# Batch 0's pooling ordered by when its loads land, output evictions shared between two engines, and a new work list

## The chip, the cores and the metric

The kernel runs on one core of a Trainium2 chip. The metric is the device time of one execution in microseconds. A core has a matrix engine (TensorE, PE in the profile, with its weight loads as PEld), three engines that read and write on-chip memory (VectorE or DVE, ScalarE or ACT, GpSimd or POOL), a queue engine (SyncE or SP) and 16 DMA engines. Engines run in their own order and wait for each other through semaphores. Matrix results go to PSUM, which has eight banks of 128 x 512 fp32 values; DVE or ACT takes them from there ("evicts" them) to SBUF.

## The reference

Four batches of 12544 rows of x with 128 features pass through an attention with 32 inducing points and then through a maxout layer:

```python
def mab(q, kv):
    s = scale * (q @ kv.transpose(0, 2, 1))
    s = s - s.max(-1, keepdims=True)
    a = np.exp(s)
    a /= a.sum(-1, keepdims=True) + 1e-09
    return a @ kv
h = mab(I, x)                  # per batch: 32 x 128, pooling over 12544 rows
attn = mab(x, h)               # 12544 x 128 again
h1, h2 = attn @ w1, attn @ w2  # 128 -> 1024
out = np.maximum(h1, h2) @ w_out
```

The output is 50176 x 128 in fp32.

## The kernel before, in words

**The algebra.** The second attention gives each row as a sum of 32 rows of h with weights e / sum(e), so `attn @ w` is `e @ (h @ w)` over the same sum. The kernel writes max(h1, h2) as relu(h2 - h1) + h1. Per batch it makes `hwd` = h (w2 - w1), 32 x 1024, and `m1` = h w1 w_out, 32 x 128. A row of the output is then (relu(e hwd) w_out + e m1) / sum(e).

**Tiling.** A batch is 98 chunks of 128 rows. Blocks take four "quarters" of up to four chunks each; quarter q lives on partitions 32q to 32q+31. `stage` (L625) computes the 32 scores of each chunk of a block into one bank, and ACT's exponential (L637) writes them as `e2`. A "phase" (`phase`, L1009) is up to four jobs, one for each quarter, that run side by side in the four 32-row strips of PE: a job multiplies `e2` by a part of `hwd` into a bank of its own, and a relu on ACT (L1024) or DVE (L1027) takes the bank to SBUF. A phase can also carry the "linear" part of a group, `e2` times `m1`, straight into the output's bank. A "group" is one quarter of one block: eight final matmuls for each chunk (L859) add relu times w_out up in one bank. Then `evict_group` multiplies by 1 / sum(e) while it writes fp32 to one of `NOUT` output buffers (L891, DVE), and SP issues the store (L918). The sums of e come from a DMA transpose and POOL's adds (`turn_e2`, L651 to L664), for the first blocks from a small matmul (`dens`, L704).

**Batch 0's pooling** runs ahead of all that, since nothing else is there to do. Its 98 chunks come in 11 loads, of 14 (four), 7 (four), 6, 5 and 3 chunks. The first part comes in fp32 over SP's queue, the others as fp16 over POOL's, followed by w1, w2 and w_out. For part i, `p1_transpose` turns the chunks on PE (L262) into two banks, of which DVE (L266) copies the first and ACT (L269) the second; `p1_scores` multiplies with the inducing points (L278), ACT takes the exponential (L287), and `p1_accum` adds up sums (L301) and h (L310). Nine warm-up matmuls run before the first load lands (L728), and `fill` puts in seven more (L720), whose results nobody reads: two inside part 0, then two, two and one behind parts 0, 1 and 2. Behind pooling come w1's negation (`w1h` times -1, DVE, L768), `small_h` (L455 on DVE, L465 on ACT), `weights_2` (eight transposes of w1, L562, copied by DVE, L565, and ACT, L568), `small_sums` (L481), the first `stage`, `small_hwd` (L501, L502, evicted by DVE, L509, and ACT, L516) and `weights_3` (L575). Pooling of batches 1 to 3 is spread through the work of the batch before, with DMA transposes of x on SP's queue (L200).

**What sets the order.** All five engines run in the order of the program text (`manual_schedule`). From L1035 on that is a list of words written out: a number is so many final matmuls, `p4.5` a phase of up to four jobs with a mask that flips the engine of its relus, `s` a stage, `gN` the sums of block N, `xB.J`, `cB.J`, `tB.J`, `aB.J` the steps of batch B's pooling, `HWmo` the small steps of batch 0's weights. While the program is built, a `Clock` keeps estimates of when each engine is free and each bank is released. With them it picks the bank for a tile, which jobs a phase takes and, but for the mask, whether ACT or DVE takes a relu:

```python
if (max(ck.act, ready) + 0.477 <= max(ck.dve, ready) + 0.597) != bool(flip >> k & 1):
    nc.scalar.activation(out=dst, in_=src, func=AF.Relu)
```

Nothing of the clock is in the program that runs, only the choices made with it. `on_act` and `on_dve` hold the entry for each instruction, `on_sp` and `st[b]["ld", i]` those for stores and loads.

Of the kernel before, what the change touches and what calls it, by code (L numbers as in the profile page):

```python
# [17 lines left out]
NOUT = 5  # L18


class Clock:
# [4 lines left out]
    LAT = 0.20  # L26
    SEM = 0.05

    def __init__(self):
        self.pe = self.act = self.dve = self.sp = 0.0  # L30
        self.pool = self.loading = self.loaded = 0.0
        self.stored = [0.0] * NOUT
        self.mode = "full"
        self.bank = [0.0] * 8
        self.idle = {}
        self.log = []
        self.busy = {}
# [86 lines left out]
def kernel(  # L124
# [57 lines left out]
    def load_x(b, i, after=None):  # L182
        k0, n = parts[b][i]
        if after is not None:

            nc.gpsimd.tensor_copy(out=pace, in_=after)
        nc.gpsimd.dma_start(out=xn_at[b, i][:, 0:n, :], in_=xr[b, :, k0 : k0 + n, :])  # L187
        if b:
            if i == 0:
                ck.loading = ck.pe  # L190
            ck.on_pool(ck.pe, 0.55)
            st[b]["ld", i] = ck.loaded = max(ck.pe, 14.0) + 8.0 + 2.7 * i
# [24 lines left out]
    w1h = relup.tile([128, 4096], F16, name="w1h", tag="relu1")[:, 0:J]  # L217
    w21 = consts.tile([C, J], F16, name="w21")
    woutp = consts.tile([128, NJB, C], F16, name="woutp")
    w1T = consts.tile([128, NJB, C], F16, name="w1T")  # L220
# [6 lines left out]
    with tc.manual_schedule(engines={ET.PE, ET.DVE, ET.Activation, ET.Pool, ET.SP}):  # L227
# [25 lines left out]
        def p1_transpose(b, i, between=0):  # L253
            k0, n = parts[b][i]
            xn = xn_at[b, i]
            h = min(8, (n + 2) // 2)
            for g, m in ((0, h), (h, n - h)):
                if g and between:
                    fill(between)
                bi, ps = bank([128, 8, 128], F16)  # L260
                for j in range(m):
                    nc.tensor.transpose(ps[:, j, :], xn[:, g + j, :], identity16)  # L262
                end = ck.run(0.056 * m, ready=ck.bank[bi], why="T")
                dst = xT_tiles[b % 2][:, k0 + g : k0 + g + m, :]
                if g == 0:
                    nc.vector.tensor_copy(out=dst, in_=ps[:, 0:m, :])  # L266
                    ck.bank[bi] = ck.on_dve(end, 0.08 + 0.075 * m)
                else:
                    nc.scalar.copy(out=dst, in_=ps[:, 0:m, :])  # L269
                    ck.bank[bi] = ck.on_act(end, 0.05 + 0.12 * m)  # L270
                st[b]["xT", i] = max(ck.bank[bi], st[b].get(("xT", i), 0.0))

        def p1_scores(b, i):
# [11 lines left out]
            end = ck.run(0.029 * n)  # L285
# [5 lines left out]
        def p1_accum(b, i, lo=0, hi=P1):  # L291
# [4 lines left out]
            if b == 0:  # L296
# [20 lines left out]
                st[0]["end"] = ck.run(0.029 * (hi - lo) + 0.03 * ((hi - lo + 3) // 4))  # L317
# [132 lines left out]
        def small_h(b):  # L450
            hT4 = smp.tile([C, 4, M], F16, name=f"hT4_{b}", tag="hT4")
            if b == 0:
# [9 lines left out]
                st[b]["hT4r"] = ck.on_dve(st[0]["end"], 0.3)  # L462
# [3 lines left out]
                ready = ck.on_act(st[0]["end"], 0.2)  # L466
# [10 lines left out]
        def small_sums(es, ready):  # L477
# [9 lines left out]
            ck.bank[st[0]["eb"]] = st[0]["rsr"] = ck.on_dve(end, 0.34)  # L487

        def small_hwd(b, halves=(0, 1), vector=False):
# [3 lines left out]
            for half in halves:  # L493
                for n in range(2 if b == 0 and half == 0 else 1):
# [25 lines left out]
                    st[b]["hw", half] = max(ck.bank[bi], st[b].get(("hw", half), 0.0))  # L520
# [35 lines left out]
        def weights_2():  # L556
            for g in range(2):
                bi, ps = bank([128, 4, 128], F16)
                ck.wait(ck.bank[bi], "w")
                for j in range(4):  # L560
                    jb = 4 * g + j
                    nc.tensor.transpose(ps[:, j, :], w1h[:, 128 * jb : 128 * (jb + 1)], identity16)  # L562
                end = ck.run(0.056 * 4)
                if g == 0:
                    nc.vector.tensor_copy(out=w1T[:, 0:4, :], in_=ps)  # L565
                    ck.bank[bi] = ck.on_dve(end, 0.4)
                else:
                    nc.scalar.copy(out=w1T[:, 4:8, :], in_=ps)  # L568
                    ck.bank[bi] = w_of["w1T"] = ck.on_act(end, 0.5)
# [162 lines left out]
        for i in range(4):  # L732
            p1_transpose(0, i, 2 if i == 0 else 0)
            if i < 3:
                fill(2 - i // 2)
            if i == 0:
                bi, ps = bank([128, 512])
                nc.tensor.transpose(ps[:, 0:M], ind_sb, identity32[0:M, 0:M])
                nc.vector.tensor_copy(out=inducingT, in_=ps[:, 0:M])
                ck.bank[bi] = 0.0  # L740
                nc.vector.reduce_sum(out=diag, in_=identity32.rearrange("p (k m) -> p m k", m=M), axis=AX.X)
                for dst, f in ((rep32, DOWN / scale), (repd, 1.0)):
                    nc.vector.tensor_scalar(
                        out=dst.rearrange("p (k m) -> p k m", m=M),
                        in0=diag[:, None, :].broadcast_to((128, 4, M)),
                        scalar1=f,
                        scalar2=None,
                        op0=ALU.mult,
                    )
            if i > 0:  # L750
                p1_accum(0, i - 1)
            p1_scores(0, i)
        last = len(parts[0]) - 1
        p1_transpose(0, 4)
        p1_accum(0, 3)
        p1_transpose(0, 5)
        p1_scores(0, 4)
        for i in range(6, last + 1):
            p1_transpose(0, i)
            p1_scores(0, i - 1)  # L760
            p1_accum(0, i - 2)
        p1_scores(0, last)
        p1_accum(0, last - 1)
        p1_accum(0, last)
# [3 lines left out]
        nc.vector.tensor_scalar(out=w1h, in0=w1h, scalar1=-1.0, scalar2=None, op0=ALU.mult)  # L768
        sums = small_h(0)
        weights_2()  # L770
        small_sums(*sums)
        stage(blocks[0])
        small_hwd(0, (0,))

# [8 lines left out]
        for n, g in enumerate(groups):  # L783
            g.blk.last_group[g.q] = n
        state.update({"g": 0, "mm": 0, "done": 0, "issued": 0})
# [95 lines left out]
        def evict_group(g, end):  # L881
# [3 lines left out]
            qs = sorted({q for q, _ in g.chunks})  # L885
            per = n // len(qs)
            t0 = g.chunks[0][1]
            rp = g.blk.rp[:, t0 : t0 + per, qs[0] : qs[-1] + 1]
            if len(qs) == 1:
                rp = rp.broadcast_to((128, per, C))  # L890
                nc.vector.tensor_mul(osb[:, 0:n, :], g.ps[:, 0 : n * C].rearrange("p (s c) -> p s c", s=n), rp)  # L891
            elif per == 1:
                rp = g.blk.rp[:, t0, qs[0] : qs[-1] + 1]
                nc.vector.tensor_mul(
                    osb[:, 0:n, :],
                    g.ps[:, 0 : n * C].rearrange("p (s c) -> p s c", s=n),
                    rp[:, :, None].broadcast_to((128, n, C)),
                )
            else:
                for i, q in enumerate(qs):  # L900
                    nc.vector.tensor_mul(
                        osb[:, per * i : per * (i + 1), :],
                        g.ps[:, per * i * C : per * (i + 1) * C].rearrange("p (s c) -> p s c", s=per),
                        g.blk.rp[:, t0 : t0 + per, q : q + 1].broadcast_to((128, per, C)),
                    )
            end = max(end, g.blk.divided, ck.stored.pop(0))
            ck.bank[g.bank] = ck.on_dve(end, 0.066 + n * 128 / 960.0)
# [13 lines left out]
        def next_job(q):  # L921
# [11 lines left out]
            if ("hw", unit[3] // unit[2]) not in st[blk.b] or relu_slot(blk, q) is None:  # L933
# [26 lines left out]
        def phase(n, flip=0):  # L960
            gl, jobs = pick(n)
            got = []
            free = sorted(range(8), key=lambda j: ck.bank[j])
            ready = 0.0
            for (q, blk, unit), bi in zip(jobs, free):
                ready = max(ready, ck.bank[bi], blk.staged, st[blk.b]["hw", unit[3] // unit[2]])
                got.append((q, blk, unit, bi, bank([128, 512], only=bi)[1]))
            if ck.mode != "row":
                keep_busy(ready - ck.SWITCH["row"])
                ck.pe += ck.SWITCH["row"]  # L970
                ck.mode = "row"
            ck.wait(ready, "phase")
            parts_ = []
            if gl is not None:
                q, b = gl.q, gl.blk.b
                r = slice(32 * q, 32 * (q + 1))
                parts_.append((q, [
# [10 lines left out]
                ]))  # L988
            for q, blk, (_, t0, w, u), bi, ps in got:
# [3 lines left out]
                parts_.append((q, [  # L993
# [10 lines left out]
                ]))  # L1004
            parts_ = [seq for _, seq in sorted(parts_, key=lambda e: e[0])]
# [4 lines left out]
            end = ck.run(0.226, "row")  # L1010
            if gl is not None:
                gl.linear = True
                if gl in held:
                    held.remove(gl)
                    evict_group(gl, end)
            for k, (q, blk, (_, t0, w, u), bi, ps) in enumerate(got):
# [5 lines left out]
                ready = end + 0.03  # L1022
# [13 lines left out]
        H0 o p4.5 s W p4.2 s 4 m0 4 p2.1 3 p3.2 1 g2 4 p2 8 p3.3 p2 14 p3.1 4 p4.1 6 x1.0 16 p2.1 p4.10  # L1036
        16 x1.1 x1.2 p4.4 4 g1 12 p4.9 12 p4.11 p1 19 p3.4 p2 14 p4 s s 3 x1.3 x1.4 4 x1.5 x1.6 7 p3.5 s
        s g3 8 p4.10 27 p3 p4.2 18 p3.2 14 p3 6 p4.4 12 x1.7 3 x1.8 x1.9 c1.0 p1 p4.4 13 g4 1 p4.5 15
# [84 lines left out]
```

## Time and profile before

| | us |
|---|---|
| median of 3 runs (317.37 to 317.73) | 317.66 |
| the profiled execution | 318.49 |
| its span, first to last instruction | 316.7 |
| batch 0's pooling, first scores to last accumulation | 8.71 to 22.48 |
| first final matmul (L859) | 26.89 |
| PE busy over the span | 311.5 |
| ACT busy, DVE busy | 279.0, 273.6 |

An execution's time is 1.8 us longer than its span. The granted clock of PE is 1.00 throughout. A row of the page's costliest groups reads: line, engine, operation, output tile and input tiles, shapes, count, then busy time and mean nanoseconds of one, then how long the engine stood idle just before, and for what. A row of the timeline begins with its start and its length in us; rows of the chain of waits with the start and the length of a link.

### The profile page before, as it was taken

Reading aid. Unit: us, or ns where it says so; the run is one execution under the profiler, and the core shown is the slowest. Engines: PE = TensorE matmul, PEld = TensorE weight load, DVE = VectorE, ACT = ScalarE, POOL = GpSimd, SP = SyncE. Lnnn points to the kernel's source line nnn. Section 1 sums busy time; section 2 is a strip of 40 time slices with the busy share of each in tenths; the row PEclk is TensorE's granted clock in tenths of the full one; section 3 lists DMA queues with packets and bytes.
Section 4 is the critical chain, followed back from the end, with each engine's and each line's share of the span. In section 5 each row is a group of like instructions: output and inputs, shape, how many; then the busy total and the mean of one; then the engine's idle time right before and its main releaser. Section 6 shows DMA issues by size and latency. Waiting matters only on the chain.

```text
span 316.7 us, 12562 instructions
## 1 busy us (share of the span) xinstructions
PE 311.5 (98%) x5309; PEld 240.8 (76%) x5309; DVE 273.6 (86%) x486; ACT 279.0 (88%) x571; POOL 127.5 (40%) x189
## 2 busy tenths in 40 slices
PE   8999999999999999999999999999999999999996
PEld 3885767777877768778777787887868777787885
DVE  2348989999888899998988998889899989989995
ACT  2669999999999999998999989999899999998881
POOL 7442071648510066067320064449305663461500
PEclk9999999999999999999999999999999999999999
DMA  8999999999699998997399998995423233324223
GB/s 205 209 206 212 226 232 213 225 239 217 120 215 244 234 175 175 198 234 205 113 216 243 179 248 212 229 187 169 139 85 118 85 120 118 119 79 146 104 103 117
DMA packets 81480, 56.34 MB, mean 178 GB/s; under 512 B 62832, under 2 KB 66064, under 8 KB 81424
## 3 DMA queue, kind: packets, MB, share of 16 engines
q1 hardware_dynamic: 75312, 41.32, 56.6%
q0 software_dynamic: 6112, 14.22, 23.1%
q8 instruction: 41, 0.67, 1.0%
q14 instruction: 15, 0.12, 0.1%
HBM read 28.33 MB, written 25.69 MB: 171 GB/s over the span
## 4 chain that ended last, share of the span: by engine, by line
PE 95%; ACT 1%; DMA 1%; DVE 1%; issue 1%; DVEq 0%; ACTq 0%
PE ps L859 61%; PE ps L1009 23%; PE ps L625 2%; PE ps L262 2%; PE ps L338 2%; PE ps L396 1%; DMA xf<-in_x_dram 1%; PE ps L278 1%; PE ps L310 1%; PE ps L720 1%; PE ps L301 1%; PE ps L505 0%; PE ps L441 0%; ACT hwd L516 0%; ACT relu L1024 0%
## 5 line engine op out<-in xcount | busy, mean ns | idle before, releaser
L1024 ACT ACTIVATE relu<-ps 128x512 f16<-128x512 f32 x472 | 242.9, 619 | 20.8 <-PE ps L1009 18.9
L1027 DVE TENSOR_SCALAR relu<-ps 128x512 f16<-128x512 f32 x312 | 198.5, 684 | 19.4 <-PE ps L1009 18.6
L859 PE MATMUL ps<-woutp,relu 128*128 128x128 f16 x3136 | 204.0, 219 | 0.0
L859 PEld LDWEIGHTS <-relu 128*128 128x128 f16 x3136 | 176.6, 98 | 34.2 <-issue 28.7
L1009 PE MATMUL ps<-e,hwd 32*128 32x512 f16 (+2 forms) x880 | 85.3, 357 | 0.0
L660 POOL TENSOR_TENSOR half<-ed 128x256 f32<-128x256 f16 (+2 forms) x23 | 14.1, 613 | 126.9 <-DMA ed<-e 126.6
L664 POOL TENSOR_TENSOR rd<-den,minus 128x16 f32<-128x16 f32 (+2 forms) x23 | 60.7, 2639 | 1.9
L891 DVE TENSOR_TENSOR o<-ps,rd 128x512 f32<-128x512 f32 (+1 forms) x88 | 55.5, 633 | 4.1 <-PE ps L1009 2.4
L1009 PEld LDWEIGHTS <-hwd 32*128 32x128 f16 x880 | 28.0, 91 | 18.4 <-issue 5.1
L1009 PE MATMUL ps<-m,e 32*128 32x128 f16 x382 | 38.5, 216 | 0.0
L1009 PEld LDWEIGHTS <-e 32*128 32x128 f16 x382 | 22.6, 92 | 5.4 <-issue 1.7
L660 POOL TENSOR_TENSOR half<-half 128x32 f32<-128x32 f32 (+3 forms) x69 | 22.3, 323 | 5.4
L187 POOL DMA_DIRECT2D xn<-in_x_dram x31 | 17.0, 557 | 7.3 <-DMA xn<-in_x_dram 4.5
L891 DVE TENSOR_TENSOR o<-ps,rp 128x512 f32<-128x512 f32 (+3 forms) x20 | 12.9, 644 | 1.1 <-DMA out_dram<-o 0.8
L266 DVE COPY xT<-ps 128x512 f16<-128x512 f16 (+3 forms) x11 | 5.5, 504 | 8.3 <-PE ps L262 8.1
L637 ACT ACTIVATE e<-ps 128x512 f16<-128x512 f32 (+2 forms) x21 | 11.0, 596 | 0.2 <-PE ps L625 0.2
L351 ACT ACTIVATE eu<-ps 128x512 f16<-128x512 f32 x18 | 11.1, 615 | 0.1
L269 ACT COPY xT<-ps 128x768 f16<-128x768 f16 (+3 forms) x11 | 6.1, 557 | 3.6 <-PE ps L262 3.4
L625 PE MATMUL ps<-xT,hT 128*32 128x512 f16 (+3 forms) x114 | 8.8, 363 | 0.1
L262 PE MATMUL ps<-identity,xn 128*128 128x128 f16 x98 | 7.8, 226 | 0.1
L262 PEld LDWEIGHTS <-xn 128*128 128x128 f16 x98 | 6.0, 101 | 1.7 <-DVE xn L724 1.0
L338 PE MATMUL ps<-xT,inducingT 128*32 128x512 f16 x72 | 7.1, 386 | 0.0
(100 smaller groups left out, 112.4 us busy)
## 6 DMA issues: line engine op xcount, KB each, us to landing
out_dram<-o SPq DMA_DIRECT2D x90, 256.0 KB, 2.7
xn<-in_x_dram POOLq DMA_DIRECT2D x24, 448.0 KB, 11.8
out_dram<-o SPq DMA_DIRECT2D x10, 128.0 KB, 2.6
xn<-in_moe_w_dram POOLq DMA_DIRECT2D x4, 256.0 KB, 14.0
xn<-in_x_dram POOLq DMA_DIRECT2D x4, 224.0 KB, 9.6
xT<-xn SPq DMA_TRANSPOSE x33, 4.4
xf<-in_x_dram SPq DMA_DIRECT2D x1, 512.0 KB, 3.7
xf<-in_x_dram SPq DMA_DIRECT2D x1, 384.0 KB, 4.2
```

Source lines behind the costliest of these rows:

```text
L187: nc.gpsimd.dma_start(out=xn_at[b, i][:, 0:n, :], in_=xr[b, :, k0 : k0 + n, :])
L262: nc.tensor.transpose(ps[:, j, :], xn[:, g + j, :], identity16)
L338: nc.tensor.matmul(out=ps[32 * g : 32 * (g + 1), :], lhsT=inducingT, rhs=xT_tiles[b % 2][:, U * u + 4 * g : U * u + 4 * (g + 1), :], start ...
L351: nc.scalar.activation(out=eu, in_=ps, func=AF.Exp, scale=scale, accum_out=st[b]["es"][:, u : u + 1])
L625: nc.tensor.matmul(out=ps[32 * q : 32 * (q + 1), 128 * t : 128 * (t + n)], lhsT=hq, rhs=xT[:, c : c + n, :], start=True, stop=True, tile_p ...
L660: nc.gpsimd.tensor_tensor(out=dst, in0=cur[:, :, 0:n], in1=cur[:, :, n : 2 * n], op=ALU.add)
L664: nc.gpsimd.tensor_tensor(out=rp[:, 0:wd, :].rearrange("p t q -> p (t q)"), in0=den[:, 0 : 4 * wd], in1=minus1[:, 0 : 4 * wd], op=ALU.pow,)
L859: nc.tensor.matmul(out=g.ps[:, 128 * c : 128 * (c + 1)], lhsT=g.blk.relu[g.q][:, 128 * (jb * w4 + t) : 128 * (jb * w4 + t + 1)], rhs=woutp ...
L891: nc.vector.tensor_mul(osb[:, 0:n, :], g.ps[:, 0 : n * C].rearrange("p (s c) -> p s c", s=n), rp)
L1009: nc.tensor.matmul(**seq[i])
L1024: nc.scalar.activation(out=dst, in_=src, func=AF.Relu)
L1027: nc.vector.tensor_scalar(out=dst, in0=src, scalar1=0.0, scalar2=None, op0=ALU.max)
```

## The change

Five things change at once.

1. **Batch 0's pooling.** A list `HEAD` spells the order out: `3a` and `3b` are the two halves of part 3's transposes, `S3` its scores, `A3` its accumulation, `I` the transposes of the inducing points and the small DVE work on them. Transposes of a part stand where the clock has them landed (`LANDED`). Five of the seven idle matmuls are gone; the two inside part 0 stay.
2. **Between pooling and the list.** `weights_2` is cut in three: the first four transposes of w1 where all eight were, the other four behind the first half of `small_hwd`, and then the two copies. The transposed w1 lives in the relu buffer that also holds w1. The list now begins with `H1` instead of `H0`: hwd's second half stands before the first phase and is evicted by DVE instead of ACT.
3. **Evictions of the output.** For each of the 108 groups a character of `EVICT` names the engine: 0 is DVE in one instruction, as before; 1 is ACT, an instruction for each chunk, with the column of reciprocals as its scale. The string has 90 zeros and 18 ones; the 18 groups have 61 chunks. (2 would share a group out and does not occur.)
4. **Six output buffers** instead of five.
5. **The clock and the list.** The clock follows a phase's four strips one by one (`ROW`, `ck.tile`), knows hwd by pieces of 256 columns, and has some other entries changed. A phase issues the linear part first instead of by quarter. The list of words is new throughout: 250 phases instead of 249; PE changes between whole-array, row-strip and column-strip matmuls 342 times instead of 348. Of the relus, ACT has 458 instead of 472, DVE 326 instead of 312. Apart from the five idle matmuls, PE's instructions are the same in number and shape.

```diff
-NOUT = 5
+NOUT = 6
...
-        def p1_transpose(b, i, between=0):
+        LANDED = [0.0, 7.5, 9.66, 11.88, 12.96, 14.02, 15.13, 17.25, 18.16, 18.97, 19.52]
+
+        def p1_transpose(b, i, half):
...
-            for g, m in ((0, h), (h, n - h)):
-                if g and between:
-                    fill(between)
+            g, m = ((0, h), (h, n - h))[half]
...
+            end = ck.run(0.0555 * m, ready=max(ck.bank[bi], LANDED[i] + 0.1), why="T")
...
-        for i in range(4):
-            p1_transpose(0, i, 2 if i == 0 else 0)
-            if i < 3:
-                fill(2 - i // 2)
...
+        p1_transpose(0, 0, 0)
+        fill(2)
+        ck.pe, ck.act = 7.18, 6.25
+        p1_transpose(0, 0, 1)
+        HEAD = """
+        1a 1b I S0 S1 2a 2b A0 A1 S2 3a 3b 4a 4b A2 S3 5a 5b S4 6a 6b S5 A3 S6 A4 A5 A6 7a 7b 8a 8b
+        S7 9a 9b S8 A7 10a 10b S9 A8 S10 A9 A10
+        """
...
         sums = small_h(0)
-        weights_2()
+        weights_2(0)
         small_sums(*sums)
         stage(blocks[0])
+        ck.wait(22.1, "w")
         small_hwd(0, (0,))
+        weights_2(1)
+        weights_2b(0)
+        weights_2b(1)
...
+            q, t0 = g.chunks[0]
+            who = int(EVICT[g.index])
+            m = (n, 0, (n + 1) // 2)[who]
...
+            if m:
                 nc.vector.tensor_mul(
...
+            for k in range(m, n):
+                nc.scalar.activation(
+                    out=osb[:, k, :],
+                    in_=g.ps[:, k * C : (k + 1) * C],
+                    func=AF.Copy,
+                    scale=g.blk.rp[:, t0 + k, q : q + 1],
+                )
+                done = max(done, ck.on_act(end, 0.165))
...
+            for q, ready in ([(gl.q, 0.0)] if gl is not None else []) + [(g[0], g[5]) for g in got]:
+                ck.issue = max(ck.issue, ck.tile[q], ready)
+                ck.tile[q] = ck.issue + ck.ROW
+                ends.append(ck.tile[q] + ck.LAT)
...
-        H0 o p4.5 s W p4.2 s 4 m0 4 p2.1 3 p3.2 1 g2 4 p2 8 p3.3 p2 14 p3.1 4 p4.1 6 x1.0 16 p2.1 p4.10
+        H1 x1.0 o p4.4 s W 4 p4.4 p2 s 4 m0 6 p3 2 p2 g2 6 p3 p2.1 13 p3 7 p4 6 x1.1 14 p2.1 p4.9 18 x1.2
...
+        EVICT = "000000000001000100001001100000100000000000000100010100000000000001001010100000000000000000010100010010000100"
```

## The prediction

> **What bounds the kernel now.** I read the page first (span, engines, chain that ended last), then busy time by stage, then the chain through the first 30 us, then ScalarE's (ACT's) timeline where its scale is a tile instead of a constant.
>
> ```profile
> span 316.7 us, 12562 instructions
> ...
> PE 311.5 (98%) x5309; PEld 240.8 (76%) x5309; DVE 273.6 (86%) x486; ACT 279.0 (88%) x571; POOL 127.5 (40%) x189
> ...
> PE 95%; ACT 1%; DMA 1%; DVE 1%; issue 1%; DVEq 0%; ACTq 0%
> ...
> L1024 ACT ACTIVATE relu<-ps 128x512 f16<-128x512 f32 x472 | 242.9, 619 | 20.8 <-PE ps L1009 18.9
> L1027 DVE TENSOR_SCALAR relu<-ps 128x512 f16<-128x512 f32 x312 | 198.5, 684 | 19.4 <-PE ps L1009 18.6
> ```
>
> The last two lines read: 472 relus on ACT keep it busy for 242.9 us, 619 ns each, and ACT stood idle for 20.8 us before them. TensorE (PE) is on 95% of the chain.
>
> Busy time by stretch (span, then PE, weight loads, DVE, ACT, POOL):
>
> ```profile
> 8.70:22.50 13.80, 13.35 (x316) 12.18 (x316) 5.78 (x14) 9.06 (x22) 6.14 (x11) 1.00 1.20 206
> 22.50:26.90 4.40, 4.32 (x59) 2.61 (x57) 3.28 (x8) 3.94 (x10) 1.61 (x3) 1.00 1.09 215
> 26.90:84.00 57.10, 57.07 (x972) 41.92 (x974) 53.52 (x93) 54.66 (x116) 25.89 (x34) 1.00 1.06 215
> ```
>
> From 26.9 us on PE is never idle, and ACT is free for only 2.4 us of 57. (The list of waits has PE's matmuls waiting for data three times, 1.8 us in all, the last at 16.1 us.) So there the time is PE's issue alone, and nothing may hold PE up. The head is different:
>
> ```profile
> 14.23 0.81 ACT xT L269
> ...
> 15.50 0.55 ACT et L287
> ...
> 21.88 0.26 ACT et L287
> ...
> 22.47 0.46 PE ps L562 x8
> ...
> 24.21 1.07 ACT hwd L516 x2
> ...
> 26.89 0.38 PE ps L859 x4
> ```
>
> This is the chain before the first final matmul (L859): pooling waits for its own copies and exponentials, ends at 22.5, and 4.4 us of small steps follow.
>
> ACT with a scale read from a tile (`rs`), and with a constant scale:
>
> ```profile
> 26.70 0.30 ACT L583 ACTIVATE w1out<-ps 128x128 f16<-128x128 f32 x1
> 26.86 1.11 ACT L1024 ACTIVATE relu<-ps 128x512 f16<-128x512 f32 x2
> ...
> 42.46 1.37 ACT L637 ACTIVATE e<-ps,rs 128x512 f16<-128x512 f32 x2
> 43.60 0.72 ACT L1024 ACTIVATE relu<-ps 128x512 f16<-128x512 f32 x1
> ...
> 88.18 2.18 ACT L637 ACTIVATE e<-ps 128x512 f16<-128x512 f32 x4
> 90.09 0.76 ACT L1024 ACTIVATE relu<-ps 128x512 f16<-128x512 f32 x1
> ```
>
> With the tile two take (43.60 - 42.46) / 2 = 0.570 us of queue each; with a constant four take (90.09 - 88.18) / 4 = 0.478. The tile costs 0.092 us an instruction. A 128x128 instruction with a constant holds the queue for 0.16 us (26.70 to 26.86).
>
> **The change, part by part.**
>
> *Idle matmuls.* Five of the seven 128x512 fills (L720) go: 5 x 0.216 = 1.08 us of PE, all of it before 12.3 us, where loads pace PE afterwards.
>
> *Pooling by landing.* The parts land at 7.50, 9.66, 11.88, 12.96, 14.02, 15.13, 17.25, 18.16, 18.97 and 19.52 us (issue plus time to landing). POOL's issue order is the same, so I keep these. I laid the new order against them with the durations of the rows: transposes 0.056 us a chunk, scores 0.025, accumulation 0.032 plus 0.04 per four chunks, PE's last issue to the evicting engine 0.21, copies 0.69 (DVE) and 0.80 (ACT) for the large halves, 0.25 to 0.37 at the end. Part 1 is ready at 7.6. Its DVE copy (8.2 to 8.9) now stands before the `inducingT` copy, so the first scores start at 9.0, not 8.71. PE then waits 0.1 to 0.5 us for parts 4, 5, 8 and 9. The last part's transposes issue at 19.7 (before: 20.70), its exponential at 20.75, and accumulation ends at 21.2, not 22.48: 1.3 us earlier. Covers of the small steps are gone there, but each only waits for a landing.
>
> *From pooling to the first final matmul.* w1 lands at 20.75 and w2 at 21.98. The negation (0.42) ends at 21.2, hT at 21.6, four weight transposes and the fp32 sum run to 21.9, the first stage's matmuls to 22.2, and the first hwd matmul comes at 22.25 (before 23.51); w2's landing is just hidden. The other four transposes and hwd's second half slip in ahead of the first phase, which comes at 23.4 (before 24.48). One phase and one stage fewer now precede L859: first final matmul at 24.7 instead of 26.89, -2.2 us. What moved behind it costs a phase (0.40) and a stage (0.35); over the whole list mode switches fall from 348 to 342 (6 x 0.095) and phases rise from 249 to 250 (0.23): +0.3 in all.
>
> *Wait added behind it.* DVE now does the first 256 of hwd, the w1T copy, hwd's second 512 and two relus in a row: 22.65 + 0.40 + 0.34, then from 23.5 three of 0.60, ends at 25.4. The second phase stands at 24.9 and its fourth tile needs the bank of the last of these relus: 0.5 us. The second q0 relu on ACT comes behind an exponential and w1out (0.2), a later bank 0.2, small ones 0.1: 1.0 us, where the old order lost 0.3 after 26.9. Net +0.7; bounds 0.2 and 1.3. Laid the same way, the old order reaches L859 at 26.55, 0.35 before the trace; like for like the step is -1.9, so the head is -1.9 + 0.3 + 0.7 = -0.9, between -1.6 (all of the 2.2, the least wait) and 0 (the full wait, pooling's gain halved).
>
> *Output evictions.* 18 of the 108 groups (61 chunks) go from DVE (L891, 0.60 us a group) to ACT, a chunk at a time, with `scale` a column of the reciprocals. No row shows this form. The nearest is 0.16 (128x128, constant) plus 0.092 for the tile: 0.25 us a chunk, 1.0 a group; the bounds are 0.16 and, with all of a lone instruction, 0.30 + 0.09 = 0.39. The new list's own entry for a chunk is 0.165 (`ck.on_act(end, 0.165)`), so 61 x 0.086 = 5.2 us of ACT time are in no entry. In exchange 14 relus move from ACT to DVE (472 and 312 become 458 and 326), so ACT gains 61 x 0.25 - 14 x 0.478 = 8.6 us of the 20.8 it had idle, and DVE gets 18 x 0.60 - 14 x 0.60 = 2.4 us lighter.
>
> How it reaches PE, in one place: group 11 (o written from ps204). After its last matmul PE has 13 final matmuls (0.73 us), a switch (0.15) and a phase (0.23); then a tile that reuses its bank: 1.11 us. ACT needs 0.21 + 3 x 0.25 + 0.39 + 0.04 = 1.39: PE waits 0.28. At 0.16 a chunk it would be 1.02, on DVE 0.93, and nobody waits. Behind the eviction stand three relus, which the next final matmuls read. With the same sum for each of the 18 groups and the relus behind it, eleven hold PE up by 0.06 to 0.3 us, 2.2 us in all. The ends are 0 (all swallowed) and 61 x 0.092 = 5.6 (all passed on); I take 2.2, since a chunk is nearest to the 0.16 and the 0.092.
>
> [...]
>
> *DMA queues.* SP issues the same 33 transposes of x and 108 stores, POOL the same loads. The new list puts batch 1's first transpose ahead of the first store: it waits for its load (landed at 25.6) and the store is due at 28.5, so nothing queues behind it. SP spends 138 us waiting for DVE's evictions, which covers its other moves: 0, and at worst the 0.6 of one store held up.
>
> *Six output buffers, w1T in a relu buffer, linear part first in a phase.* DVE waited 0.9 us in all for a store (`o L891 <- DMA out_dram`), and PE never for that: -0.1 to 0, I take 0. The relu buffer is free again after L575, before it is wanted. The order in a phase moves no matmul count: 0. Tail (313.8 to 316.7): last eviction and store, same: 0.
>
> **Sum.** -0.9 + 2.2 = +1.3 us. The profiled execution took 318.49 us (span 316.7 and 1.8 around it), 0.8 above the median of 317.66, so it becomes 319.8, and the median 319.0.
>
> **Rivals.**
> 1. ACT's idle time swallows the tile's cost. For it: 20.8 us idle before its relus, and evictions that have a whole group to finish. Against: the idle time is in 50 pieces of 0.4 us (18.9 us), each about one group's extra 0.37, and lies where the relus wait for a phase, not where an eviction stands. Time: -0.9, 316.8 us. It decides if under 0.26 us of the 5.6 reach PE.
> 2. Part of it is swallowed, 0.3 to 1.5 us: within 0.2%, 317.0 to 318.3.
> 3. The order does not do what it says: the landings come later, or the new chain behind 21.2 loses what pooling won. Head 0, 319.9 us.
> 4. Nearly all of ACT's extra time is passed on, 5.6 - 0.9 = +4.7: 322.4.
> 5. Without fills PE's clock drops. The first warm matmuls ran 427 ns and those after 7.5 us 216, so a slow state exists. In the new pooling PE has some 10 us of work, and twice that would be +10 at most, +2 if a fifth of it ran slow: 320.9 us. Against: PE's longest gap there is 0.5 us. [...]
>
> **Numbers.** Forecast 0.45 (319.0; own range 318.3 to 320.7), rival 1 0.18, rival 2 0.17, rival 3 0.10, rival 4 0.07, rival 5 0.03. 0.2% is 0.64 us, about what a measurement of this kernel can tell from no change. Faster 0.18, same 0.17, slower 0.65. The range runs from rival 1 (half of it lies lower) to halfway between the forecast and rival 4: 316.7 to 320.7; under and over it lie about 0.09 each.
>
> **What the profile after would show.** Accumulation's end near 21.2 and first final matmul near 24.7 (head right); a wait of about 0.5 us in the second phase, ending with a DVE relu; evicting ACTIVATEs at 0.25 us steps; PE pauses of 0.1 to 0.3 us where a phase follows an ACT eviction, some 2 us in all. I am wrong if these steps are 0.16, or if they are 0.25 and PE shows no pause.

## The result and the profile after

The changed kernel takes 322.2 us in the middle of four runs (321.86 to 322.27), the kernel before 317.7 beside it: 1.0137 times as long, interval 1.0119 to 1.0155. Run again beside later experiments, it was 1.0145 (1.0128 to 1.0163). It is 4.5 us slower where 1.3 were forecast. Its profiled execution took 322.27 us, span 320.5.

The page of the changed kernel: span, busy times, the chain's engines and the two groups of relus, as for the kernel before, and the new evictions on ACT (busy time, mean ns, idle time before).

```profile
span 320.5 us, 12614 instructions
...
PE 312.0 (97%) x5304; PEld 239.9 (75%) x5304; DVE 273.0 (85%) x483; ACT 286.1 (89%) x617; POOL 127.5 (40%) x189
...
PE 85%; DMA 5%; ACT 5%; DVE 2%; issue 1%; POOL 1%; SPq 0%; ACTq 0%; POOLq 0%; DVEq 0%
...
L1044 ACT ACTIVATE relu<-ps 128x512 f16<-128x512 f32 x458 | 235.8, 624 | 15.2 <-PE ps L1029 13.7
...
L913 ACT ACTIVATE o<-ps,rd 128x128 f32<-128x128 f32 x57 | 17.1, 400 | 2.8 <-issue 2.8
```

PE held 95% of the chain and now holds 85%; DMA and ACT have taken 5% each. ACT had 20.8 us of idle time before its relus and has 15.2. By stretch, with the same columns as before:

```profile
8.70:22.50 13.80, 12.24 (x301) 11.22 (x300) 5.62 (x16) 9.02 (x22) 6.21 (x11) 1.00 1.20 206
22.50:26.90 4.40, 4.22 (x60) 2.66 (x60) 3.44 (x10) 3.35 (x7) 1.61 (x3) 1.00 1.09 214
26.90:84.00 57.10, 56.24 (x920) 41.15 (x919) 52.02 (x88) 54.81 (x119) 25.89 (x34) 1.00 1.04 215
```

In pooling PE is busy for 12.2 us of 13.8 where it was for 13.35: it stands and waits. Between 26.9 and 84 it did 972 matmuls and does 920. The chain through the head shows where:

```profile
5.34 10.91 DMA xn<-in_x_dram
16.25 0.04 issue
16.30 0.57 PE ps L265 x7
...
22.23 0.09 PE ps L313 x3
22.32 0.23 PE ps L564 x4
...
25.18 1.21 DVE relu L1047 x2
26.39 0.04 issue
26.43 0.48 PE ps L1029 x7
...
26.93 0.61 ACT relu L1044
27.54 0.05 issue
27.58 0.40 PE ps L874 x4
```

The sixth load on POOL's queue landed at 16.25 us; in the profile before it had landed at 15.13. PE's list of waits has this one at 1.1 us. So accumulation ended at 22.3, 0.15 earlier than before and not 1.3. The first final matmul is at 25.55 (predicted 24.7, before 26.89); the chain's last row above is the next four. Behind it come the two predicted waits: the second phase for a DVE relu (0.44 us from one matmul's start to the next, of which 0.18 stands in PE's timeline as idle; 0.5 was predicted) and the next final matmul for an ACT relu (0.37, of which 0.29 stands in PE's list of waits).

What the evictions do, at the place that the prediction named (group 11). ACT's timeline in the changed kernel, then PE's:

```profile
61.47 1.14 ACT L913 ACTIVATE o<-ps,rd 128x128 f32<-128x128 f32 x4
62.50 2.06 ACT L1044 ACTIVATE relu<-ps 128x512 f16<-128x512 f32 x4
```

```profile
62.04 0.39 PE L1029 MATMUL ps<-e,hwd 32*128 32x512 f16 x4
62.27 0.21 PE L1029 MATMUL ps<-m,e 32*128 32x128 f16 x1
62.27 0.76 PE L1029 MATMUL ps<-e,hwd 32*128 32x512 f16 x3
62.67 0.34 PE L1029 MATMUL ps<-m,e 32*128 32x128 f16 x3
```

Four chunks start 0.249 us apart and hold the queue from 61.47 to 62.50. The second phase reuses the evicted bank: its three large matmuls start at 62.27 and last until 63.03, and the linear part's other three come at 62.67 instead of right behind 62.27. PE stood for 0.38 us; 0.28 was predicted.

### The profile page after: what moved, and what is told of

The parts are those of the page before. It is cut to its first block, busy times and chain, and to the rows that moved or that the text cites. A ratio compares the mean times of both kernels' runs of the same rounds, so it can differ in the third digit from the quotient of the medians.

```text
span 320.5 us, 12614 instructions
## 1 busy us (share of the span) xinstructions
PE 312.0 (97%) x5304; PEld 239.9 (75%) x5304; DVE 273.0 (85%) x483; ACT 286.1 (89%) x617; POOL 127.5 (40%) x189
## 4 chain that ended last, share of the span: by engine, by line
PE 85%; DMA 5%; ACT 5%; DVE 2%; issue 1%; POOL 1%; SPq 0%; ACTq 0%; POOLq 0%; DVEq 0%
PE ps L874 55%; PE ps L1029 22%; DMA xn<-in_x_dram 3%; ACT relu L1044 3%; PE ps L632 2%; PE ps L341 2%; ACT o L913 1%; DMA xT<-xn 1%; PE ps L399 1%; DVE relu L1047 1%; POOL xn L189 1%; PE ps L313 1%; PE ps L265 0%; DVE o L906 0%; PE ps L304 0%
## 5 line engine op out<-in xcount | busy, mean ns | idle before, releaser
L1044 ACT ACTIVATE relu<-ps 128x512 f16<-128x512 f32 x458 | 235.8, 624 | 15.2 <-PE ps L1029 13.7
L1047 DVE TENSOR_SCALAR relu<-ps 128x512 f16<-128x512 f32 x326 | 206.2, 683 | 24.4 <-PE ps L1029 23.0
L1029 PE MATMUL ps<-e,hwd 32*128 32x512 f16 (+2 forms) x880 | 87.7, 357 | 0.2 <-DVE relu L1047 0.2
L906 DVE TENSOR_TENSOR o<-ps,rd 128x512 f32<-128x512 f32 (+2 forms) x71 | 45.3, 639 | 2.9 <-ACT o L913 1.3
L1029 PE MATMUL ps<-m,e 32*128 32x128 f16 x382 | 39.3, 217 | 0.0
L1029 PEld LDWEIGHTS <-e 32*128 32x128 f16 x382 | 23.3, 93 | 10.6 <-issue 2.9
L667 POOL TENSOR_TENSOR half<-half 128x32 f32<-128x32 f32 (+3 forms) x69 | 22.3, 323 | 5.4
L913 ACT ACTIVATE o<-ps,rd 128x128 f32<-128x128 f32 x57 | 17.1, 400 | 2.8 <-issue 2.8
L906 DVE TENSOR_TENSOR o<-ps,rp 128x512 f32<-128x512 f32 (+3 forms) x19 | 12.2, 640 | 0.9 <-PE ps L874 0.9
L632 PE MATMUL ps<-xT,hT 128*32 128x512 f16 (+3 forms) x114 | 8.4, 362 | 0.0
```

The costliest lines, as they stand in the source:

```text
L632: nc.tensor.matmul(out=ps[32 * q : 32 * (q + 1), 128 * t : 128 * (t + n)], lhsT=hq, rhs=xT[:, c : c + n, :], start=True, stop=True, tile_p ...
L667: nc.gpsimd.tensor_tensor(out=dst, in0=cur[:, :, 0:n], in1=cur[:, :, n : 2 * n], op=ALU.add)
L906: nc.vector.tensor_mul(osb[:, 0:m, :], g.ps[:, 0 : m * C].rearrange("p (s c) -> p s c", s=m), g.blk.rp[:, t0 : t0 + m, q : q + 1].broadcas ...
L913: nc.scalar.activation(out=osb[:, k, :], in_=g.ps[:, k * C : (k + 1) * C], func=AF.Copy, scale=g.blk.rp[:, t0 + k, q : q + 1],)
L1029: nc.tensor.matmul(**seq[i])
L1047: nc.vector.tensor_scalar(out=dst, in0=src, scalar1=0.0, scalar2=None, op0=ALU.max)
```

## What takes the time: ACT's evictions

**The tile scale taken away.** ACT's evictions with a constant scale:

```diff
-                    scale=g.blk.rp[:, t0 + k, q : q + 1],
+                    scale=1.0,
```

> The 61 output evictions on ACT keep their place and order but take a constant scale of 1.0 instead of a column of the reciprocals (the division is left out for these 18 groups). 61 x 0.092 = 5.6 us of ACT time go, nothing else moves. Theory A (the pauses of PE behind ACT's evictions come from the tile's extra time, 2.2 us by the prediction): laid out with the rows' durations, the pauses after 28 us fall from 3.2 to 0.9, so about 2.3 us less, near 319.9. Rival B (the loss lies in the list, the head and the transposes of x, and the idle time of ACT would have swallowed the tile): less than 0.7 us, 321.5 or more. Rival C (nearly all of ACT's time is passed on): 4.5 us or more less, below 317.7.

Measured: 318.6 us (10 runs), 1.0024 of the kernel before (1.0012 to 1.0036), so 3.6 us less than the changed kernel. Theory A, with a larger share than it gave: 64% of the 5.6 us. PE at group 11 in this run:

```profile
61.72 0.39 PE L1029 MATMUL ps<-e,hwd 32*128 32x512 f16 x4
61.95 0.21 PE L1029 MATMUL ps<-m,e 32*128 32x128 f16 x1
61.95 0.38 PE L1029 MATMUL ps<-e,hwd 32*128 32x512 f16 x3
62.00 0.33 PE L1029 MATMUL ps<-m,e 32*128 32x128 f16 x3
```

The 0.76 is 0.38 and the wait is gone. Both kernels issue the same matmuls in the same order, so the n-th can be compared in the two traces. The changed kernel falls 3.5 us behind between 50 and 310 us, in steps. The largest are at 62.7 (0.38 us), 304 (0.34), 93 (0.32), 225 (0.29) and 215 (0.27); sixteen are over 0.12.

**A second tile operand.**

```diff
-                    func=AF.Copy,
+                    func=AF.Identity,
+                    bias=zero,
                     scale=g.blk.rp[:, t0 + k, q : q + 1],
```

> The 61 output evictions on ACT read a second tile operand, a bias of zeros (Identity instead of Copy; the values are the same), so each takes another 0.09 us: 61 x 0.092 = 5.6 us more on ACT. The constant scale took 3.6 us off the changed kernel's time. Theory A (the idle time of ACT covers a share that is soon used up, so more of the second 5.6 us is passed on than of the first): 4.5 to 5.6 us more, 326.7 to 327.8. Rival B (a constant share, 64%): 3.6 more, 325.8. Rival C (the cost of the first operand was not its duration but something that happens once, as a late bank): under 2 us more, below 324.2.

Measured: 327.2 us (326.6 to 327.5), 1.0296 of before (1.0274 to 1.0317): 5.0 us more than the changed kernel. Theory A. ACT's group of evictions, whose mean of 400 ns became 487:

```profile
L915 ACT ACTIVATE o<-ps,zero,rd 128x128 f32<-128x128 f32 x57 | 22.2, 487 | 2.9 <-issue 2.9
```

Chunks started 0.158, 0.249 and 0.342 us apart with none, one and two tile operands, so the first adds 91 ns and the second 93. Of the first 5.6 us PE got 3.6, of the second 5.0. What idle time covers is used up by the first 0.09 us of a chunk; of the second 0.09 us nine tenths reach PE.

**The same groups on DVE.** One `tensor_mul` for a group, at the list's places:

```diff
-            if m:
-                nc.vector.tensor_mul(osb[:, 0:m, :], ...)
-            for k in range(m, n):
-                nc.scalar.activation(...)
+            nc.vector.tensor_mul(osb[:, 0:n, :], ...)
```

> The changed kernel with the 18 groups evicted by DVE, one instruction of 0.60 us each, and everything else where the list has it, so ACT is 15 us lighter and DVE 10.8 us heavier. Theory A (the list has moved relus to DVE in exchange, so DVE has no room at these places: laid out with the rows' durations, the pauses after 28 us grow from 3.2 to 7): 3 to 5 us slower than the changed kernel, 325 to 327. Rival B (DVE's 24 us of idle time before its relus hold the 10.8, and the loss was only ACT's): near the run with a constant scale, 318.6.

Measured: 325.2 us, 1.0230 (1.0209 to 1.0252), 3.0 slower than the changed kernel: theory A, at its lower end. In PE's list of waits the bank that DVE has not yet evicted stands first (total, times, longest):

```profile
PE ps L1023 <- DVE o L905: 1.4, 4, 0.8
...
PE ps L1023 <- DVE relu L1041: 0.5, 3, 0.2
```

So ACT was not the wrong engine for this list, which has also moved 14 relus to DVE. Both engines still have idle time before their relus (15.2 us on ACT and 24.4 on DVE in the changed kernel), but not at these places: time that the planning does not know comes out at PE there on either engine.

**Five groups on ACT.** 13 groups go back to DVE, a chunk is entered at its measured 0.25, and 41 relus change engine. The hole in the head and the transposes of x, below, are mended too:

```diff
-                done = max(done, ck.on_act(end, 0.165))
+                done = max(done, ck.on_act(end, 0.25))
...
-                if (max(ck.act, ready) + 0.477 <= max(ck.dve, ready) + 0.597) != bool(flip >> k & 1):
+                if RELU[state["issued"]] == "A":
```

> The changed kernel with five groups instead of 18 on ACT, a chunk entered at 0.25 us instead of 0.165, 41 of the 784 relus changed to the other engine to balance (469 on ACT, 315 on DVE), the hole in batch 0's order filled and the two transposes of x early; PE's order behind the pooling is the new list's. Theory A (the loss was the evictions' 3.6 us, the transposes' 0.7 and the standstill's 0.5, and the new list itself is as good as the old): pauses of PE as in the run with a constant scale, 316.6 to 317.7, at or just under the kernel before. Rival B (the list itself is worse): 318.0 to 319.0.

Measured: 318.3 us (11 runs), 1.0015 (1.0004 to 1.0027). The 4 us come back, but the time lies in rival B's range, at its lower end: with the three losses mended the new list is still no better than the old. No version here beats the kernel before.

## What takes the time: transposes of x

```diff
-        ... x1.3 6 p3.6 s s s s 6 g3 5 ... x1.4 4 x1.5 ...
+        ... x1.3 y1.4 y1.5 6 p3.6 s s s s 6 g3 5 ... x1.4 4 x1.5 ...
```

(`y` sends the transpose; `x` then only keeps the clock's books.)

> The changed kernel with two of batch 1's DMA transposes (x1.4 and x1.5) issued right behind x1.3, ahead of two stores and of one transpose of e, instead of behind them; nothing else moves. Theory A (the first scores of batch 1 hold PE up by 0.89 us at 55.4 us, since their transpose was issued at 51.1 instead of 46.9): that step goes, 0.6 to 0.9 us less, near 321.4. Rival B (the two stores held up there cost an output buffer and give it back, or the next transpose is late in its place): within 0.3 us of the changed kernel.

Measured: 321.5 us, 1.0116 (1.0099 to 1.0134), 0.7 less than the changed kernel: theory A. The two intervals overlap, so it is the trace that decides. The chain of the changed kernel, then of this run:

```profile
51.07 4.26 DMA xT<-xn
55.33 0.04 issue
55.37 0.38 PE ps L341
```

```profile
53.49 1.05 PE ps L883 x17
54.54 0.33 PE ps L350 x4
```

The scores of batch 1 had waited for `x1.4`, which stood behind two stores and a transpose of e on SP's queue. Compared matmul by matmul, the two traces part by 0.89 us at that one place and nowhere else behind the head.

**Five output buffers.**

```diff
-    outp = ctx.enter_context(tc.tile_pool(name="outp", bufs=NOUT))
+    outp = ctx.enter_context(tc.tile_pool(name="outp", bufs=5))
```

> The changed kernel with five output buffers in place of six; nothing else moves. Prediction's step (six buffers are worth 0): within 0.3 us of the changed kernel. Rival (the first store takes 14.2 us to land behind the transpose of x, where it took 6.4 before, so the sixth buffer is what keeps the evictions going): 0.4 us or more slower, with DVE or ACT waiting for a store.

Measured: 322.4 us (321.96 to 323.23), 1.0142 (1.0119 to 1.0166), no difference in the median. But one execution, the profiled one at 323.23, shows the rival at work:

```profile
30.52 13.98 DMA out_dram<-o
...
44.59 0.70 DVE o L906
...
45.33 0.51 PE ps L632 x8
```

The first store took 14 us to land behind the first transpose of x, DVE waited 1.7 us for its buffer and PE 1.6 for DVE; 0.9 of it came back at the scores that waited for `x1.4` anyway. Set beside the changed kernel's trace, this one also reaches its first final matmul 0.59 us later, since PE's granted clock was 0.50 from 18.2 to 21.6 us (last section); of the 0.96 us between the two times the buffer is thus the smaller part. In the changed kernel that transpose took 18.2 us (25.71 to 43.95) and the store behind it landed at 44.14; before, the first store needed 6.4. With six buffers no engine waits for a store there. What the sixth buffer is worth without the new place of the transpose was not tried. (The two landings are 0.2 us apart in the changed kernel and 1.1 with five buffers.)

## What the head is worth

**The pooling alone, both ways.** The old order and seven fills in the changed kernel, and the new order with two fills in the kernel before; behind the pooling nothing moves:

```diff
-        1a 1b I S0 S1 2a 2b A0 A1 S2 3a 3b 4a 4b A2 S3 5a 5b S4 6a 6b S5 A3 S6 A4 A5 A6 7a 7b 8a 8b
+        F2 I S0 1a 1b F2 A0 S1 2a 2b F1 A1 S2 3a 3b A2 S3 4a 4b A3 5a 5b S4 6a 6b S5 A4 7a 7b S6 A5
```

> The changed kernel with the old order of batch 0's pooling and its seven idle matmuls; the rest of the list, the banks and the engines are as in the changed kernel. Theory A (the sixth of the loads landed at 16.25 us instead of 15.13, and the new order stands still for it, so the new order won nothing in this execution): within 0.3 us of the changed kernel if that load lands near 16.25 again, 0.6 us slower if it lands near 15.1. Rival B (the new order is worth 1.3 us whatever lands when, and the loss lies behind it): 1.0 to 1.5 us slower than the changed kernel. Rival C (the new order itself costs): faster by more than 0.3 us.

> The kernel before with the new order of batch 0's pooling and two idle matmuls instead of seven; the list and all behind the pooling are as before. Theory A: -0.6 us where the sixth load lands near 15.1 us, 0 where it lands near 16.2; so between 0 and -0.6 against the kernel before, 317.1 to 317.7. Rival B (worth 1.3 us): 316.4. Rival C (it costs, the clock of PE or a copy on the wrong engine): above 318.0.

Measured: 322.0 us (1.0127, 1.0108 to 1.0147) and 318.15 (1.0007, 0.9993 to 1.0020). The sixth load landed at 16.55 and 16.35. Neither way does the new order win or lose anything that can be measured. In the first that is theory A's value for a late landing. In the second the median lies above theory A's range and just inside rival C's; the ratio, 0.2 us, does not tell it from no change.

**The hole filled.** Other work stands ahead of the late load's transposes:

```diff
-        S4 6a 6b S5 A3 S6 A4 A5 A6 7a 7b 8a 8b
+        S4 A3 S5 6a 6b A4 S6 A5 7a 7b A6 8a 8b
```

> The changed kernel with one piece of batch 0's order moved: the accumulation of part 3, the scores of part 5 and the accumulations of parts 4 and 5 are issued around the transposes of part 6 so that PE has work until that part's load lands (5a 5b S4 A3 S5 6a 6b A4 S6 A5 7a 7b A6 8a 8b); nothing behind the pooling moves. Theory A (the sixth load lands at 16.2 to 16.5 us in nearly every execution, as in four of the five new traces, and the order written for 15.13 stands still there): 0.5 to 0.8 us less than the changed kernel, first final matmul about 0.7 earlier. Rival B (what is won before the end of pooling is waited for again behind it, at w2's landing near 22.1 and at hwd): less than 0.2 us.

> The kernel before with the new pooling and two idle matmuls, and with PE given work until the sixth load lands (the order of the run with the hole filled); all behind the pooling is as before. The new order alone gave 1.0007 of the kernel before. Theory A (only the standstill at the sixth load took the order's gain): 0.3 to 0.8 us less than the kernel before, 316.9 to 317.4. Rival B (what is won is waited for again behind it, at w2's landing near 22.1 or at the fp32 sum): within 0.2 us of the kernel before.

> The changed kernel with the hole in batch 0's order filled and the two transposes of x issued early, the evictions as they are. Theory A (the two losses are separate and add): 1.0 to 1.5 us less than the changed kernel, 320.7 to 321.2. Rival B (the time won in the head is waited for again at the next transposes of x, which land when the loads let them): 0.7 less, 321.5.

> The changed kernel once more, beside the others of this call: 322.0 to 322.4 by both theories, with the sixth load landing at 16.0 to 16.5 us and a step of about 1.1 us there.

Measured: in the changed kernel 322.0 us (1.0137, 1.0113 to 1.0161); in the kernel before 317.84 (1.0003, 0.9989 to 1.0017); with the transposes of x 321.8 (1.0127, 1.0107 to 1.0147); the changed kernel beside the last two 322.4, its load at 16.28. The profiles show what was meant: the first final matmul comes at 25.01 instead of 25.55, and at 24.73 with both mended. The medians do not follow. In the kernel before, the interval of 12 runs leaves at most 0.35 us of theory A's 0.3 to 0.8. In the changed kernel four runs spread over 1.3 us and settle little: the profiled one kept its 0.54 us to the end and is the fastest of the four (321.46). Rival B's number is near in all three, but the places that it named for the first two (w2's landing, the fp32 sum, hwd) lie ahead of the first final matmul, where the lead is still there. With both mended, the chain shows another place:

```profile
61.86 6.12 DMA xT<-xn
...
68.03 0.21 PE ps L374 x2
...
71.78 4.45 DMA eT<-eu
...
76.28 0.63 PE ps L408 x32
```

Batch 1's last transpose of x lands at 67.98, about when it did in the run without the mended hole (67.81). PE, now ahead, waits 0.74 us for it and then 0.33 for a transpose of exponentials. Up to 77 us PE can thus meet transfers that do not come earlier because PE does.

**The execution that the prediction was built on.** Two more profiled executions each of the kernel before and of the kernel before with the hole filled:

> The kernel before, looked at again. Its profiled execution took 318.49 us, its other runs 317.66 in the middle. Theory A (executions of one kernel differ in the head, by when the loads land and how PE meets them, and are the same behind it): first final matmul at 25.8 to 26.5 instead of 26.89 where the execution is near 317.6, and PE's pauses behind 30 us as before. Rival B (they differ in the steady part, as by the 0.4 to 0.6 us lost near 105 to 108 us): first final matmul again near 26.9, the difference behind it. Rival C (in the stores at the end): last matmul at 313.8, a shorter tail than 2.95 us.

> As the look before: the same kernel, for the spread between two executions on one chip. Theory A: where the first final matmul comes x us earlier, the end comes x us earlier. Rival B: the two are not tied.

> The kernel before with the hole-filled pooling, whose profiled execution reached the first final matmul at 25.78 (kernel before: 26.89) and took 317.39, while the middle of its 12 runs was 317.84. Theory A: the first final matmul moves between executions by half a us or more, so the old order's typical one is near 26.0 and the new order wins little. Rival B: again near 25.8 and 1.1 ahead of the old order's, with the gain lost between there and the end.

> As the look before, for the spread. Theory A: the end follows the first final matmul, us for us. Rival B: it does not.

Measured: 317.32 and 317.27 us for the kernel before, with the first final matmul at 25.94 and 26.09 and the last matmul at 312.60 and 312.55 (profile before: 26.89 and 313.78); 317.73 and 317.17 with the hole filled, first final matmul at 25.63 and 25.77. Theory A holds for the head: in both new executions the old order's is 0.8 to 0.95 us shorter than in the first, and the new one's lead shrinks to 0.3. Us for us the end does not follow, which is rival B of the second executions: with the hole filled, the one that is ahead at 25.63 ends later, since it lost 0.4 us each near 205 and 216 us to transposes of exponentials. Where the 0.8 arises, in the chain of the kernel before as first profiled and in the next execution:

```profile
5.27 1.03 PE ps L262 x8
6.30 0.83 PE ps L720 x2
...
8.71 0.30 PE ps L278 x6
```

```profile
5.28 0.62 PE ps L262 x8
5.90 0.45 PE ps L720 x2
...
7.91 0.50 PE ps L278 x14
```

The same eight transposes and two fills take 1.86 us in one execution and 1.07 in the other. PE went over from 427 to 216 ns a fill at about 7.0 us in the first and by 5.3 in the second; over all the traces with nine warm matmuls it does so anywhere from 4.3 to 7.2, with the first matmul at 1.2 each time. What sets the moment is not shown. The granted clock on the profile's page is 1.00 in both and does not show this start at half rate; the time from one matmul to the next does.

**The rate set by hand.** One warm matmul instead of nine, in either kernel:

```diff
-    WARM = 9
+    WARM = 1
```

> The kernel before with one warm matmul instead of nine ahead of batch 0, so that PE's busy stretch begins at 5.3 us instead of 1.2; nothing else changes. In the looks at this kernel PE's matmuls went from 427 to 216 ns at about 5.3 us (317.3 us) and at 7.0 us (318.5 us). Theory A (the old order has PE on its path from 5.3 us to the end of pooling, so every matmul at half rate is paid): the change of rate comes at 8.7 to 12 us, accumulation ends 1.5 to 3 us later than 21.5, and the time rises as much, 319 to 320.7. Rival B (the rate at the start decides nothing, the difference between the looks came with the loads): within 0.3 us of 317.7.

> The changed kernel with one warm matmul instead of nine. Theory A (in the new order PE stands waiting for loads, 0.9 us at part 1 and 1.1 at part 6, and the sixth load at 16.2 us sets the end of pooling): the slow matmuls fill those waits, accumulation ends within 0.4 us of 22.2 and the time stays within 0.5 us of 322.3, so the new order is the less sensitive of the two. Rival B: it rises as much as the kernel before with one warm matmul does.

Measured: the kernel before 319.3 us beside 317.3 (1.0063, 1.0039 to 1.0087), 2.0 us more; the changed kernel 322.1 (1.0144, 1.0119 to 1.0169), nothing. Theory A's times in both. The old order has PE on its path from 5.3 us on and pays for the slow matmuls (accumulation 2.3 us later than in the two later executions above). In the changed kernel with one warm matmul accumulation ends at 21.9, but not by the order alone: the sixth load landed early (15.19; 15.32 in the other kernel). And the first final matmul comes at 26.60, 1.05 us later than with nine, because PE ran at half rate again from 22.3 to 25.7 us (last section). Set beside the trace with nine, this one is still 0.84 us behind at 43 us and has it back at the scores that wait for `x1.4`. So the equal time is theory A's number, but the wait that swallowed the loss is that of the transposes.

## Why the prediction was right and wrong

- **Right: direction and mechanism.** It is slower, ACT evicts at 0.249 us a chunk (0.25 predicted, 0.165 in the list), PE pauses where a phase takes the bank, and the second phase waits 0.44 us (0.5).
- **Evictions, +2.2: mis-sized.** They cost 3.6. "Eleven hold PE up by 0.06 to 0.3 us" were sixteen of 0.13 to 0.38: group 11 came to 0.38 where the sum gave 0.28. Where the sums had the other five as covered, they were short too; that each missed a latency of group 11's 0.1 us would do it, but was not traced.
- **DMA queues, "0, and at worst the 0.6 of one store": failed.** 0.7 us. The text looked at the first transpose and its store, which the sixth buffer covered. It did not follow the transposes `x1.4` and `x1.5`, issued at 51.07 and 53.01 us where they were at 48.31 and 49.88 before, to the scores that read them.
- **Head, -0.9: failed in its landings and its baseline.** "POOL's issue order is the same, so I keep these" took 15.13 us for the sixth load; of 19 further profiles 17 have it at 16.0 to 16.6, and two, those with one warm matmul, at 15.2 and 15.3. The gain was counted from an accumulation that ended at 22.48, which was late because PE's rate changed late. (Its +0.3 for what moved behind the first final matmul also adds up to 0.4 from its own terms; that changes nothing here.)
- **"The median is 0.8 lower": failed.** The 0.8 was the slow start of that one execution. The changed order does not feel it, so there was nothing to subtract: four traces with its head whose rate changed at 6.6 to 7.2 us reach the first final matmul at 25.36 to 25.45, the two of the changed kernel, at 4.3 and 5.5 us, at 25.55 and 25.57.
- **Six buffers, w1T in a relu buffer, the phase's order, 0:** the buffers right in the median (322.4 with five), though in the one trace with five PE waited 1.6 us for the 14-us store; the other two were not tried alone and lie in the remainder below.

Together, against the median before, 4.5 us were measured: 3.6 for the tile scale, 0.7 for the transposes, and a remainder of 0.2 for head and list, which no run measures by itself (318.6 - 0.7 is 317.9, where the kernel before has 317.66). The forecast had +2.2, 0 and -0.9. Rival 4 named nearly the right time, 322.4, by the wrong sum: not all of the 5.6 us, but 3.6 and two losses of another kind. Rival 3 was right on the landing, rival 1 (all swallowed) is refuted by the run with a constant scale, and rival 5's drop of the rate is not in the changed kernel's profile (216 ns a fill at 6 us), but two traces of the last section have it, and 21 of the 84 executions with the new order have the mean clock that goes with it. It did not make the 4.5 us: the granted clock is 1.00 in all four executions behind the 322.2.

## What to carry to other kernels

Where several engines are planned to the tenth of a microsecond, an entry 0.09 us too low can be paid at the bottleneck, here at two thirds at first (3.6 of 5.6 us) and nearly whole once the slack was gone (5.0 of the next 5.6); price the exact form of an instruction, operands included. A landing or a start read from one execution is a sample: before an order is tuned to it, or a gain counted from it, profile two or three more. When work is moved in a list, follow every DMA that moves with it to the instruction that reads its result, not only to what stands behind it in its queue.

## What was not expected of the hardware

PE's matmuls fell back to half speed in the changed kernel with one warm matmul, with no wait of PE for data over 0.4 us in its list behind 5.3 us. The chain of that run:

```profile
22.12 0.31 PE ps L484 x2
22.44 0.55 PE ps L632 x4
...
24.38 0.43 PE ps L504
24.81 0.43 PE ps L505
```

A 512-wide matmul (L504, L505) takes 0.43 us here and 0.22 in the changed kernel, and the stage's four (L632) 0.55 instead of 0.33, from about 22.3 to 25.7. Nine warm matmuls do not prevent it. The run with five buffers, which has the changed kernel's head, shows the same (span, PE and the other engines as above; the number behind the five engines is the granted clock):

```profile
14.77:18.18 3.41, 2.45 (x70) 2.27 (x67) 0.85 (x2) 2.25 (x6) 2.20 (x4) 1.00 1.17 204
18.18:21.59 3.41, 3.39 (x60) 3.34 (x57) 1.22 (x4) 1.74 (x6) 1.95 (x4) 0.50 1.32 199
```

Both drops last 3.41 us, and both begin 13.65 us, four times 3.41, after the clock had first risen (at 4.53 and 8.64 us). So the traces can be cut into stretches of 3.41 us from that rise, and the columns that PE streams in each can be added up, at the 0.42 ns a column of a 216-ns fill. The stretch ahead of the drop comes to 0.34 and 0.36 of its length in the two traces with a drop; in the other 18 none of the first five stretches is below 0.37, and with the old order's pooling none is below 0.46. So both drops come behind a stretch in which PE streams less than in any of those of the other traces, but the margin is 0.01, and that the one causes the other is a guess, which two drops do not prove. If it does, the standstill at the sixth load and the missing fills cost more than the idle time. Of 84 executions with the new order 21 have a mean granted clock of 0.995 or less, which is what one drop to 0.50 for 3.41 us makes of 320 us, and of more than 60 with the old order none has. Their cost is small beside the rest: leaving them out moves the medians of the two kernels with the old list and the new pooling (12 runs each) by less than 0.1 us.

The DMA transposes of x are the other surprise: one of 14 x 128 columns or less took 3.1 to 5.7 us to land when issued between 50 and 80 us in the changed kernel (6.1 with hole and transposes mended), and the one issued at 25.71 us, while the loads of batch 1 were under way (they landed from 25.70 to 39.88), took 18.2. The store issued behind it at 29.93 landed at 44.14, after it.
